# Columns 256 to 511 of x's first 512 rows: eight TensorE transposes replaced by one transposing DMA, and two broadcasts moved behind the Silu table

## Chip, cores and metric

The kernel runs on one core of a Trainium2 chip. The metric is the device time of one launch in microseconds (us). Its engines are TensorE (PE; its weight loads are shown as PEld), VectorE (DVE), ScalarE (ACT), GpSimd (POOL) and SyncE (SP). DMAs are issued from SP's and ACT's instruction queues and are moved by 16 DMA engines.

## What is computed

A gate mixes two branches over the same x (2048 rows of 448 columns, bf16): a diagonal complex state space model, and a dense layer pair with Silu.

```python
g = sigmoid((x * gate_w).sum(-1, keepdims=True))
# branch a
dt      = exp(log_dt)
Lam_bar = exp(dt * (Lambda_re + 1j * Lambda_im))
Bu      = einsum("bld,pd->blp", x, ((Lam_bar - 1) / Lam)[:, None] * Bmat)
h_t     = Lam_bar * h_{t-1} + Bu_t             # 2048 steps
a       = 2 * einsum("blp,dp->bld", h, Cmat).real + x * Dskip
# branch b
b = einsum("bsf,fd->bsd", silu(einsum("bsd,df->bsf", x, w1)), w2)   # 448 -> 1792 -> 448
out = g * a + (1 - g) * b
```

## The kernel before

Two successive rows of x are taken as one row of 896 columns (`x2`, 1024 rows): columns 0 to 447 are the even time steps, 448 to 895 the odd ones. The matmuls need x with its columns on partitions. That is `XT`, eight blocks of 128 columns by 1024 rows: blocks 0 to 3 for the even steps (block 3 holds columns 384 to 511, of which the lower 64 belong to the even steps), 4 to 7 for the odd ones. The recurrence is done on pairs of steps, and the w1 product ("ffn1") is done in four quarters of 512 rows (two of even steps, two of odd ones), each with 14 blocks of 128 hidden columns, written two PSUM banks at a time. Silu empties two banks at once into `AT` (L455).

The Tracker (L43) records every operation in program order, one list for each engine, and puts a wait on a semaphore ahead of an operation that reads or writes what another engine or a DMA has last touched. An engine's order is thus the order of the calls, and a waiting instruction holds up whatever stands behind it on its engine. The order is written by hand. DMAs to the keys R0 and R1 share one semaphore, and R2 has another.

The start, in which the change lies:

- **x, first 512 rows.** `XH` is their natural form, with four groups of 128 rows. SP and ACT load columns 0 to 255 of groups 0 and 1 (L276), then columns 0 to 383 of groups 2 and 3 (L280, keys XA2 and XA3), then the rest up to column 511 (keys XB0 and XB1, L282 and L286). PE turns 128x128 pieces (`turn_k`, L489 to L493; the instruction is L491) into PSUM, and DVE copies them to `XT` (L501, L507). So arise blocks 0 to 3 for rows 0 to 511. The eight turns of blocks 2 and 3 stand at L531 and L535.
- **Other XT blocks.** They come by transposing DMAs on SP (`ldt`, L228 and L229), from L309 on, behind a wait for the remainder rows of w1 (L308).
- **w1** goes to `W1E` in pieces: for the first 768 hidden columns by j (128 columns of x each, `ld_w`), a remainder of 64 rows (`ld_wr`), and the further columns (`ld_w3`).
- **Parameter rows.** log_dt, Lambda_re and Lambda_im are loaded into rows of `R` (L283; two from SP, one from ACT). DVE copies 64 columns to R's end (`rd`, L466). PE turns R into columns (`mm_cols`, L472), DVE copies them out to `PV` (L528), and from there come dt (L565, an Exp), two small DVE operations, `mag` (L569, another Exp), and, on ACT, a dummy Silu that loads the Silu table (L572). In the table of the profile such small operations are named by their helpers: L562 for ACT, L556 and L559 for DVE.
- **ffn1, first part.** `ffn1_first` (L427, matmuls at L433) does six hidden blocks in six banks, over j = 0, 1, 2. It is a generator that stops in between, so that turns stand among its matmuls; j = 2 comes last and reads block 2. `mm_cols` stands after three of the six matmuls of j = 1. Then come the remainders (`ffn1_rem`, L447), which read block 3 and `XR`, a copy of block 3's lower half in the upper partitions, each followed by a Silu of two banks (L455). After that ffn1 goes on in pairs through `lanes` (L365), the first of them in the two free banks, the next in the two that the first Silu empties.
- **Row broadcasts.** `ld_b` (L297) loads gate_w and Dskip to all partitions (`GWB`, `DB`), issued by ACT (L300, L301) behind a dummy Exp (L292) that loads the Exp table. They are first used in `gate` (L650) and `skip` (L658), where DVE multiplies x by them.
- **Natural x.** `load_xn(0)` (L303, SP) brings columns 512 to 895 of the first 512 rows.

Of the kernel before, what the change touches and what calls it, by code (L numbers as in the profile page):

```python
# [8 lines left out]
AF = mybir.ActivationFunctionType  # L9

F32 = DT.float32
BF16 = DT.bfloat16
# [138 lines left out]
def gated_mix(nc, A_x, A_Lambda_re, A_Lambda_im, A_B_re, A_B_im, A_C_re, A_C_im, A_log_dt,  # L151
              A_Dskip, B_x, B_w1, B_w2, gate_w, out):
    with ExitStack() as ctx:
        E = ctx.enter_context
        T = Tracker(nc, ctx)

        def sb(name, shape, dtype):
            return E(nc.sbuf_tensor(name, list(shape), dtype))

        x2 = A_x[0].rearrange("(k i) d -> k (i d)", i=2)  # L160
        out2 = out[0].rearrange("(k i) d -> k (i d)", i=2)

        XT = sb("XT", [128, 8, NK], BF16)
# [7 lines left out]
        XR = sb("XR", [128, NK], BF16)  # L171
# [4 lines left out]
        XN = sb("XN", [128, 2 * NKT * D], BF16)  # L176
        AT = [sb(f"AT{i}", [128, NFB, 512], BF16) for i in range(2)]
        OT = sb("OT", [128, 4, D], BF16)
        GWB = sb("GWB", [128, D], BF16)
        DB = sb("DB", [128, D], BF16)  # L180
        JK = sb("JK", [128, 2], BF16)
# [7 lines left out]
        ID = sb("ID", [128, 128], BF16)  # L189
# [5 lines left out]
        HP = sb("HP", [128, 1], F32)  # L195
# [25 lines left out]
        ps = E(nc.psum_tensor("ps", [128, 8, 512], F32))  # L221
# [3 lines left out]
        def ld(eng, dst, src, key, group=None):  # L225
            return T.dma(eng, lambda e: e.dma_start(dst, src), writes=[key], group=group)  # L226

        def ldt(dst, src, key, reads=(), group=None, also=()):  # L228
            return T.dma("sp", lambda e: e.dma_start_transpose(dst, src), reads=reads,  # L229
                         writes=[key, *also], group=group)  # L230
# [4 lines left out]
        def swap_xr(eng, h, odd):  # L235
            hs = slice(h * 512, (h + 1) * 512)
            if odd:
                T.op(eng, lambda e: e.tensor_copy(XR[0:64, hs], XT[64:128, 7, hs]), reads=XO[h][1],
                     writes=[f"XR{h}b"])
            else:  # L240
                T.op(eng, lambda e: e.tensor_copy(XR[64:128, hs], XT[0:64, 3, hs]), reads=XE[h][1],
                     writes=[f"XR{h}a"])
# [7 lines left out]
        def row(v):  # L250
            return v.rearrange("(o n) -> o n", o=1)

        XH = XN[:, 0:8 * D].rearrange("p (k c) -> p k c", k=4)
        XA = ["XA0", "XA1", "XA2", "XA3", "XB0", "XB1"]
        FA, FB = 768, 1280
        x0 = x2[0:512, 0:512].rearrange("(k p) c -> p k c", p=128)

        def ld_w(eng, j, f0=0, f1=FA, key=""):
            ld(eng, W1E[:, j, f0:f1], B_w1[j * 128:(j + 1) * 128, f0:f1], f"W1Ej{j}{key}")
# [4 lines left out]
        def ld_w3(eng, j0, j1, f0, f1, key):  # L264
            ld(eng, W1E[:, j0:j1, f0:f1], B_w1[j0 * 128:j1 * 128, f0:f1].rearrange("(j p) f -> p j f", p=128),
               f"W1E{key}{j0}")

        def ld_wr(eng, c, later):
            p = slice(64 * c, 64 * c + 64)
            if later:  # L270
                return ld(eng, W1E[p, 3, 384:896].rearrange("p (n f) -> p n f", n=2),
                          B_w1[384:448, FA:].rearrange("p (n c f) -> p n c f", n=2, c=2)[:, :, c, :], f"W1Es{c}")
            return ld(eng, W1E[p, 3, 0:384], B_w1[384:448, 384 * c:384 * c + 384], f"W1Er{c}")

        for k, eng in enumerate(("sp", "act")):
            ld(eng, XH[:, k, 0:256], x0[:, k, 0:256], XA[k])  # L276
        for c, eng in enumerate(("sp", "act")):
            ld_w(eng, 0, 384 * c, 384 * c + 384, c)
        for k, eng in ((2, "sp"), (3, "act")):
            ld(eng, XH[:, k, 0:384], x0[:, k, 0:384], XA[k])  # L280
        ld_w("sp", 1)
        ld("act", XH[:, 0:2, 256:512], x0[:, 0:2, 256:512], XA[4])  # L282
        for i, (eng, v) in enumerate((("sp", A_log_dt), ("sp", A_Lambda_re), ("act", A_Lambda_im))):  # L283
            ld_row(eng, i, v)
        ld_w("act", 2)
        ld("sp", XH[:, 2:4, 384:512], x0[:, 2:4, 384:512], XA[5])  # L286
        gE = [ld_wr(eng, c, False) for c, eng in enumerate(("sp", "act"))]
        ld_w3("sp", 0, 2, FA, FB, "d")
        ld_w3("act", 2, 3, FA, FB, "d")
        for c, eng in enumerate(("sp", "act")):  # L290
            ld_wr(eng, c, True)
        T.op("act", lambda e: e.activation(JK[:, 0:1], HP[:, :], AF.Exp), reads=["HP"], writes=["JK0"])  # L292
        ld_w3("sp", 0, 1, FB, F_FF, "e")
        ld_w3("act", 1, 3, FB, F_FF, "e")
        BTK = [f"BT{i}" for i in range(4)] + ["BTz"]
# [1 line left out]
        def ld_b(dst, src, key):  # L297
            ld("act", dst[:, :], row(src).partition_broadcast(128).rearrange("p o n -> p (o n)"), key)

        ld_b(GWB, gate_w, "GW")  # L300
        ld_b(DB, A_Dskip, "DB")  # L301

        def load_xn(h):  # L303
            c0 = 0 if h else 512
            ld("sp", XN[:, 8 * h * D:8 * (h + 1) * D].rearrange("p (k c) -> p k c", k=4)[:, :, c0:],
               x2[h * 512:(h + 1) * 512, c0:].rearrange("(k p) c -> p k c", p=128), f"XN{h}")

# [5 lines left out]
        for i, src in enumerate((A_B_re, A_B_im)):  # L313
# [15 lines left out]
             writes=["IOTA"])  # L329
# [128 lines left out]
        def ffn1(c, f0=0, ahead=None):  # L458
            for fb in range(f0, NFB, 2):
                pair(*ffn1_pair(c, fb), last=(c == 3 and fb == NFB - 2))  # L460
                if ahead and fb == 8:
                    ahead()
                yield
# [13 lines left out]
        def warm(n, b):  # L477
            def mm(pe):
                ins = None
                for _ in range(n):  # L480
                    ins = pe.matmul(ps[:, b, 0:128], ones, ones, start=True, stop=True)
                return ins
            T.op("pe", mm, writes=[f"ps{b}"])

        warm(NWARM, 5)
        PB = (6, 7, 6, 7)
        xp = [ps[:, b, 0:256].bitcast(BF16) for b in PB]

        def turn_k(j, k, b=None):  # L489
            b = PB[j] if b is None else b  # L490
            T.op("pe", lambda pe: pe.transpose(  # L491
                ps[:, b, 0:256].bitcast(BF16)[:, k * 128:(k + 1) * 128], XH[:, k, j * 128:(j + 1) * 128], ID[:, :]),
                reads=[XA[k if j < 2 or (j == 2 and k > 1) else 4 + k // 2], "ID"], writes=[f"ps{b}"])  # L493

        def turn_x(j, i):
            for k in (2 * i, 2 * i + 1):
                turn_k(j, k)
# [6 lines left out]
        def turned_x(j, i=None, b=None):  # L504
            c, key = (slice(0, 512), f"XTe0{j}") if i is None else (slice(256 * i, 256 * i + 256), f"XTe0{j}{i}")
            b = PB[j] if b is None else b
            T.op("dve", lambda e: e.tensor_copy(XT[:, j, c], ps[:, b, 0:256].bitcast(BF16)[:, c]),  # L507
                 reads=[f"ps{b}"], writes=[key])
# [13 lines left out]
        for k in (2, 3):  # L522
# [5 lines left out]
        T.op("dve", lambda e: e.tensor_copy(  # L528
            PV[:, :, :], ps[:, 7, 256:288].rearrange("p (t c) -> p t c", c=8)[:, :, 0:4]),
            reads=["pv", "ps7"], writes=["PV"])  # L530
        for i in range(2):  # L531
            turn_x(2, i)
        turned_x(2)
        next(first)
        for i in range(2):  # L535
            turn_x(3, i)

        names = {}

        def pc(n):  # L540
            if n not in names:
                names[n] = len(names)
            return names[n]

        def col(n):
            i = pc(n)
            return P[:, i, :]
# [7 lines left out]
        def pts(o, a, s1, s2, op0, op1, ra):  # L555
            T.op("dve", lambda e: e.tensor_scalar(col(o), a, s1, s2, op0, op1), reads=ra, writes=[o])  # L556

        def ptt(o, a, b, op, ra):
            T.op("dve", lambda e: e.tensor_tensor(col(o), a, b, op), reads=ra, writes=[o])  # L559

        def pact(o, a, f, ra, scale=1.0, bias=0.0):
            T.op("act", lambda e: e.activation(col(o), a, f, bias=bias, scale=scale),  # L562
                 reads=ra, writes=[o])
# [3 lines left out]
            col("phf"), LIM, 1.0 / TWO_PI, col("dt"), ALU.mult, ALU.mult), reads=["PV", "dt"], writes=["phf"])  # L567
        ptt("ar", col("dt"), LRE, ALU.mult, ["dt", "PV"])
        pact("mag", col("ar"), AF.Exp, ["ar"])  # L569
        turned_x(3)  # L570
        T.op("dve", lambda e: e.tensor_copy(XR[64:128, 0:512], xp[3][0:64, :]), reads=["ps7"], writes=["XR0a"])
        T.op("act", lambda e: e.activation(JK[:, 0:1], HP[:, :], AF.Silu), reads=["HP"], writes=["JK0"])  # L572
        pts("phr", col("phf"), MAGIC, -MAGIC, ALU.add, ALU.add, ["phf"])
        ptt("fr", col("phf"), col("phr"), ALU.subtract, ["phf", "phr"])
        pts("nfr", col("fr"), -1.0, None, ALU.mult, ALU.bypass, ["fr"])
# [6 lines left out]
            reads=["f2"] + SGN, writes=["f2s"])  # L582
# [55 lines left out]
        def xblock(b):  # L638
            v = XN[:, 4 * b * D:4 * (b + 1) * D].rearrange("p (k c) -> p k c", k=4) if b > 1 else \
                XH[:, :, b * D:(b + 1) * D]  # L640
            return v, [*(XA if b < 2 else []), *([f"XN{b // 2}"] if b else [])]

        def block(tile):
            return tile // 4 if tile > 7 else tile % 2
# [10 lines left out]
        def skip():  # L655
            for b in range(4):
                v, ks = xblock(b)
                T.op("dve", lambda e, v=v: e.tensor_tensor(  # L658
                    v, v, DB[:, :].unsqueeze(1).to_broadcast([128, 4, D]), ALU.mult),
                    reads=ks + ["DB"], writes=[f"XD{b}"] + ks)  # L660
                yield
# [12 lines left out]
             writes=["BTz"] + BTK[2:4])  # L674
# [486 lines left out]
        f = ffn1(2)  # L1161
# [100 lines left out]
```

## Time and profile before

| | us |
|---|---|
| three timed runs, median (lowest to highest) | 136.64 (136.61 to 136.76) |
| profiled execution | 136.72 |
| its span | 135.3 |
| PE busy | 131.9 (97%) |
| DVE busy | 114.2 (84%) |
| ACT busy | 93.7 (69%) |
| POOL busy | 15.1 (11%) |

The profile is of one execution. The span runs from its first to its last instruction, and times in the trace count from the span's start. A row gives start, length, engine, source line, operation, what is written and read, and in brackets how long the engine had been idle and what ended that. "SPq" and "ACTq" are the issue of a DMA from that queue; the time to landing counts from the start of the issue. "PEld" can run ahead of PE. The chain that ended last is followed back from the last instruction through whatever released each step. Matmul records are pipelined: the lengths of two may overlap, so in the chain only the part that pushes the end is counted.

### The profile page before, as it was taken

What the parts mean: (1) busy time and instruction counts of PE and PEld (TensorE: products, weight loads), DVE (VectorE), ACT (ScalarE), POOL (GpSimd) and SP (SyncE); (2) the same over time, 40 slices, a digit from 0 to 9 for tenths busy, and PEclk for the clock granted to TensorE, in tenths of its full rate; (3) what the DMA queues carried; (4) which work ended last, traced back from release to release, by engine and by line L of the source; (5) the groups of instructions that cost most, each with busy time, mean ns of one, the idle gap of its engine ahead of it and who ended that gap; (6) DMA issues with size and microseconds to landing.
All of it is one profiled execution on the core that took longest, in us unless ns stands there. A gap on an engine that the chain in (4) does not pass through costs nothing.

```text
span 135.3 us, 2630 instructions
## 1 busy us (share of the span) xinstructions
PE 131.9 (97%) x1072; PEld 65.7 (49%) x1073; DVE 114.2 (84%) x152; ACT 93.7 (69%) x146; POOL 15.1 (11%) x32
## 2 busy tenths in 40 slices
PE   7899999999999999999999999999999999999993
PEld 7554444444444554444445544445555555555552
DVE  1467898917899798999999999999999999994554
ACT  0369888899939999768999597797113437879200
POOL 7108768050000000000000000000000000000000
DMA  4999979999897220000122000000000000222123
GB/s 109 273 278 162 157 153 244 181 286 300 251 184 123 55 62 0 0 0 0 44 56 60 5 0 0 0 5 0 0 0 0 0 0 7 100 89 81 68 78 126
DMA packets 24928, 11.95 MB, mean 88 GB/s; under 512 B 16851, under 2 KB 24406, under 8 KB 24918
## 3 DMA queue, kind: packets, MB, share of 16 engines
q1 hardware_dynamic: 22996, 10.43, 32.3%
q10 hardware_dynamic: 1922, 1.37, 3.6%
q8 instruction: 8, 0.13, 0.4%
q14 instruction: 2, 0.02, 0.0%
HBM read 5.51 MB, written 1.84 MB: 54 GB/s over the span
## 4 chain that ended last, share of the span: by engine, by line
PE 94%; DMA 3%; DVE 1%; ACTq 1%; issue 0%
PE ps L365 44%; PE ps L794 16%; PE ps L809 16%; PE ps L1047 15%; DMA XN<-in_A_x_dram 3%; PE ps L433 3%; DVE TMPS L1071 1%; ACTq L226 1%; PE ps L491 1%; PE ps L447 1%; PE ps L472 0%
## 5 line engine op out<-in xcount | busy, mean ns | idle before, releaser
L365 PE MATMUL ps<-XT,W1E 64*128 64x512 bf16 x325 | 41.3, 376 | 0.0
L455 ACT ACTIVATE AT<-ps 128x1024 bf16<-128x1024 f32 x28 | 28.2, 1019 | 7.4 <-PE ps L365 7.2
L365 PEld LDWEIGHTS ps<-XT,W1E 64*128 64x128 bf16 x325 | 16.9, 94 | 19.0 <-ACT AT L455 0.3
L365 PE MATMUL ps<-XT,BT 64*128 64x512 bf16 x156 | 22.4, 376 | 0.0
L809 PE MATMUL ps<-W,AT 64*128 64x448 bf16 x224 | 21.5, 349 | 0.0
L794 PE MATMUL ps<-W,AT 128*128 128x448 bf16 x112 | 21.4, 353 | 0.0
L794 PEld LDWEIGHTS ps<-W,AT 128*128 128x128 bf16 x112 | 10.9, 98 | 10.5 <-issue 0.4
L809 PEld LDWEIGHTS ps<-W,AT 64*128 64x128 bf16 x224 | 10.9, 94 | 10.4
L838 ACT ACTIVATE BT<-ps,GT 128x448 bf16<-128x448 f32 x8 | 5.1, 634 | 13.2 <-PE ps L794 13.2
L894 DVE SCALAR_TENSOR_TENSOR HS<-VE,P,ps 128x512 bf16<-128x512 bf16 (+1 forms) x13 | 9.6, 780 | 3.9 <-PE ps L365 3.9
L365 PEld LDWEIGHTS ps<-XT,BT 64*128 64x128 bf16 x156 | 8.1, 94 | 9.3 <-DVE HS L894 0.4
L938 DVE TENSOR_TENSOR_SCAN G<-P,Q 128x1024 f32<-128x1024 f32 (+1 forms) x6 | 11.4, 1923 | 0.0
L1047 PE MATMUL ps<-CO,VE 128*128 128x448 bf16 (+2 forms) x63 | 11.1, 332 | 0.0
L1047 PE MATMUL ps<-CO,HS 128*128 128x448 bf16 x56 | 11.1, 352 | 0.0
L365 PE MATMUL ps<-XR,W1E 64*128 64x512 bf16 x25 | 9.2, 376 | 0.0
L1047 PEld LDWEIGHTS ps<-CO,VE 128*128 128x128 bf16 x63 | 6.0, 98 | 4.8
L1047 PEld LDWEIGHTS ps<-CO,HS 128*128 128x128 bf16 x56 | 5.5, 98 | 5.1
L891 DVE TENSOR_TENSOR Q<-G,COS 128x2048 bf16<-128x2048 f32 (+1 forms) x4 | 7.0, 1755 | 0.1
L891 DVE TENSOR_TENSOR Q<-G,SIN 128x2048 bf16<-128x2048 f32 (+1 forms) x4 | 7.0, 1750 | 0.0
L856 ACT ACTIVATE VE<-ps 128x1024 bf16<-128x1024 f32 x6 | 6.1, 1020 | 1.2 <-PE ps L365 1.2
L858 ACT ACTIVATE ps<-VE,P 128x1024 f32<-128x1024 bf16 x6 | 6.7, 1118 | 0.2
L894 DVE SCALAR_TENSOR_TENSOR VE<-HS,P,FP 128x512 bf16<-128x512 bf16 (+1 forms) x7 | 6.6, 976 | 0.1
(123 smaller groups left out, 179.1 us busy)
## 6 DMA issues: line engine op xcount, KB each, us to landing
W<-in_B_w_dram SPq DMA_DIRECT2D x2, 784.0 KB, 6.6
XN<-in_A_x_dram SPq DMA_DIRECT2D x1, 896.0 KB, 5.1
out_dram<-OT SPq DMA_DIRECT2D x8, 112.0 KB, 1.7
out_dram<-TMPS SPq DMA_DIRECT2D x7, 112.0 KB, 1.7
HS<-HS SPq DMA_DIRECT2D x4, 128.0 KB, 2.3
XN<-in_A_x_dram SPq DMA_DIRECT2D x1, 384.0 KB, 3.7
W1E<-in_B_w_dram SPq DMA_DIRECT2D x1, 256.0 KB, 5.5
W1E<-in_B_w_dram ACTq DMA_DIRECT2D x1, 256.0 KB, 5.0
```

The source lines that it names most:

```text
L365: ins = pe.matmul(ps[:, bank, :], w(p, j), xh(odd, h, j, p), start=start and j == js[0], stop=stop and j == js[-1], skip_group_check=seeded)
L433: T.op("pe", lambda pe, fb=fb, bank=bank, j=j, h=h, c=c: pe.matmul(ps[:, bank, c], W1E[:, j, ff(fb) * 128:(ff(fb) + 1) * 128], XT[:, j, c] ...
L455: T.op("act", lambda e: e.activation(a[:, fb:fb + n, :], ps[:, bank:bank + n, :], AF.Silu), reads=[f"ps{bank + i}" for i in range(n)], wri ...
L794: ins = pe.matmul(ps[:, bank, 0:D], a[:, fb, q * 128:(q + 1) * 128], W2[:, ff(fb), :], start=(first and fb == 0), stop=(fb == NFB - 1), sk ...
L809: ins = pe.matmul(ps[:, bank, 0:D], a[p, fb, q * 128:(q + 1) * 128], W2[p, ff(fb), :], start=(start and fb == 0), stop=(not start and fb = ...
L838: T.op("act", lambda e: e.activation(bs(tile), ps[:, bank, 0:D], AF.Copy, scale=sc), reads=[f"ps{bank}", "GT2" if h else "GRI"], writes=ks)
L856: T.op("act", lambda e: e.activation(VE[:, m:m + 2, hs], ps[:, b[0]:b[0] + 2, :], AF.Copy), reads=[f"ps{i}" for i in b], writes=vs)
L858: T.op("act", lambda e: e.activation(ps[:, o[0]:o[0] + 2, :], VE[:, m:m + 2, hs], AF.Copy, scale=c1("lr", pt)), reads=vs + ["lr"], writes= ...
L891: T.op("dve", lambda e: e.tensor_tensor(o, a, b, op), reads=reads, writes=writes)
L894: T.op("dve", lambda e: e.scalar_tensor_tensor(o, a, s, b, ALU.mult, ALU.add), reads=reads, writes=writes)
L938: T.op("dve", lambda e: e.tensor_tensor_scan(G[:, c, w], rb, Q1[:, c, w], init, ALU.mult, ALU.add), reads=[f"Q1{c}", "rr", f"G{c}"], write ...
L1047: ins = pe.matmul(ps[:, bank, c], state(kt, odd, m), CO[:, m, c], start=False, stop=(m == YB[-1]), skip_group_check=True)
```

## The change

Columns 256 to 511 of the first 512 rows no longer come by the loads XB0 and XB1 and the eight turns. One transposing DMA on SP writes blocks 2 and 3 of `XT` (two blocks by 512 columns) directly from x in memory. It stands behind the w1 piece of j = 1 and ahead of the two parameter rows that SP issues. The loads XA2 and XA3 shrink to columns 0 to 255; the natural form of columns 256 to 511 comes later, with `load_xn(0)`, so that the first block of `gate` and `skip` waits for that load too. `XR`'s copy is taken from `XT` instead of PSUM. On ACT the dummy Exp moves from behind the w1 loads of the remainder and of the columns 768 to 1279 to directly behind the piece of j = 2, and the two broadcasts move behind the dummy Silu.

```diff
-        XA = ["XA0", "XA1", "XA2", "XA3", "XB0", "XB1"]
+        XA = ["XA0", "XA1", "XA2", "XA3"]
...
         for k, eng in ((2, "sp"), (3, "act")):
-            ld(eng, XH[:, k, 0:384], x0[:, k, 0:384], XA[k])
+            ld(eng, XH[:, k, 0:256], x0[:, k, 0:256], XA[k])
         ld_w("sp", 1)
-        ld("act", XH[:, 0:2, 256:512], x0[:, 0:2, 256:512], XA[4])
+        ldt(XT[:, 2:4, 0:512], x2[0:512, 256:512], "XTe02", also=["XTe03"])
         for i, (eng, v) in enumerate((("sp", A_log_dt), ("sp", A_Lambda_re), ("act", A_Lambda_im))):
             ld_row(eng, i, v)
         ld_w("act", 2)
-        ld("sp", XH[:, 2:4, 384:512], x0[:, 2:4, 384:512], XA[5])
+        T.op("act", lambda e: e.activation(JK[:, 0:1], HP[:, :], AF.Exp), reads=["HP"], writes=["JK0"])
         gE = [ld_wr(eng, c, False) for c, eng in enumerate(("sp", "act"))]
...
-        T.op("act", lambda e: e.activation(JK[:, 0:1], HP[:, :], AF.Exp), reads=["HP"], writes=["JK0"])
...
-        ld_b(GWB, gate_w, "GW")
-        ld_b(DB, A_Dskip, "DB")
-
         def load_xn(h):
-            c0 = 0 if h else 512
+            c0 = 0 if h else 256
...
-        for i in range(2):
-            turn_x(2, i)
-        turned_x(2)
         next(first)
-        for i in range(2):
-            turn_x(3, i)
...
         pact("mag", col("ar"), AF.Exp, ["ar"])
-        turned_x(3)
-        T.op("dve", lambda e: e.tensor_copy(XR[64:128, 0:512], xp[3][0:64, :]), reads=["ps7"], writes=["XR0a"])
+        swap_xr("dve", 0, 0)
         T.op("act", lambda e: e.activation(JK[:, 0:1], HP[:, :], AF.Silu), reads=["HP"], writes=["JK0"])
+        ld_b(GWB, gate_w, "GW")
+        ld_b(DB, A_Dskip, "DB")
```

The rest follows from this: `PB` keeps banks 6 and 7 for blocks 0 and 1, `turn_k` waits for `XA[k]` alone, and `xblock(0)` waits for `XN0` as well.

## Prediction

> **What bounds the kernel now.** I read the chain that ended last first. The profiled execution took 136.72 us, of which 135.3 us are the span; the median of the three timed runs is 136.64, so 0.08 is taken off at the end. Seen whole, the chain says that TensorE (PE) sets the end:
>
> ```profile
> PE 94%; DMA 3%; DVE 1%; ACTq 1%; issue 0%
> ```
>
> In order of time, its first dozen microseconds look otherwise (start, length, what):
>
> ```profile
> 1.71 3.59 DMA XN<-in_A_x_dram
> 5.30 0.05 issue
> 5.34 0.23 PE ps L491
> 5.57 0.22 PE ps L433 x2
> 5.79 0.11 PE ps L491 x2
> 5.90 1.47 PE ps L433 x9
> 7.37 0.08 PE ps L472 x4
> 7.45 0.24 PE ps L491 x4
> 7.69 0.05 issue
> 7.75 0.59 PE ps L433 x2
> 8.34 0.22 PE ps L491 x4
> 8.56 1.29 PE ps L433 x6
> 9.86 0.76 PE ps L447 x6
> 10.61 31.76 PE ps L365 x294
> ```
>
> The eight transposes that go are the two "L491 x4" entries, 0.24 and 0.22 us. From 10.61 on there is no gap in PE until 132.76: a microsecond won or lost before that arrives whole at the end. So the question is only when the L365 stream can run.
>
> PE is not alone in deciding that. The timeline of the other engines (start, length, idle before it and what ended the idle time):
>
> ```profile
> 6.27 0.17 DVE L466 COPY R<-R 3x64 bf16<-3x64 bf16 x1
> 7.49 0.17 DVE L528 COPY PV<-ps 128x16 f32<-128x16 f32 x1 [1.04 <-PE ps L472]
> 7.69 0.21 ACT L562 ACTIVATE P<-PV 128x4 f32<-128x4 f32 x1 [0.58 <-DVE PV L528]
> 8.33 0.20 ACT L562 ACTIVATE P<-P 128x4 f32<-128x4 f32 x1 [0.43 <-DVE P L559]
> 8.56 1.28 ACT L572 ACT_TABLE_LOAD   x1
> 9.85 0.20 ACT L572 ACTIVATE JK<-HP 128x1 bf16<-128x1 f32 x1
> 10.22 1.94 ACT L455 ACTIVATE AT<-ps 128x1024 bf16<-128x1024 f32 x2 [0.17 <-PE ps L447]
> 11.30 1.19 PEld L365 LDWEIGHTS ps<-XT,W1E 64*128 64x128 bf16 x13 [0.32 <-ACT AT L455]
> ```
>
> This is a second path: three parameter rows land in R, DVE copies (6.27), PE turns them into columns (L472), PV, an Exp, two DVE operations, a second Exp, the Silu table load, and only then the first Silu that empties PSUM banks (10.22). PE's fifth ffn1 pair needs those two banks: its weights load at 11.30, released by ACT. ACT sat idle a mere 0.17 us ahead of 10.22. **The parameter path has 0.17 us of slack**, and the transposes that go lie behind L472, beside that path. What is taken from PE there can bring at most 0.17 us.
>
> **The change, part by part.**
>
> *Transposes and evacuations out.* PE loses 0.24 + 0.22 = 0.46 us of chain, DVE three copies of 0.42 us against a new one of 0.29 (the row of L241, which now fills the upper half of XR from XT). Worth up to 0.17 us by the slack above.
>
> *Smaller loads.* The third and fourth x loads fall from 96 to 64 KB, and 128 and 64 KB go. The fourth, issued at 1.71 and landed at 5.30, is on the chain; PE was idle 0.44 us for it. Between nothing and that 0.44 is won at PE; I take 0.2, provided nothing later binds.
>
> *The transposing load (T below) on SP.* The queue before:
>
> ```profile
> 2.16 0.43 SPq L226 DMA_DIRECT2D W1E<-in_B_w_dram  x1
> 2.64 0.33 SPq L226 DMA_DIRECT2D R<-in_A_log_dt_dram  x1
> 3.01 0.22 SPq L226 DMA_DIRECT2D R<-in_A_Lambda_re_dram  x1
> 3.27 0.41 SPq L226 DMA_DIRECT2D XN<-in_A_x_dram  x1
> 8.60 3.94 SPq L229 DMA_TRANSPOSE XT<-in_A_x_dram  x2
> ```
>
> T stands at 2.64, ahead of two of the three parameter rows and of four W1 loads. First its issue: 1.26 to 2.39 us each for the six into XT. T should take about 1.5, so the rows are issued at 4.2 and 4.5 in place of 2.64 and 3.01. Second, its data lie ahead of the rows. In this trace the loads of one queue land in the order of issue, and a small one waits for what precedes it: on SP the 192 KB of W1 issued at 2.16 land at 5.86, the 64 KB of x issued at 3.27 not before 7.27 (4.0 us, where the first 64 KB took 2.1), the 48 KB of W1 issued at 3.73 at 8.63. The DMA share is 0.94 to 1.00 from 2 to 10 us: nothing passes quickly.
>
> When do the rows land (call it t_R)? Before, by 6.27. **Low end:** issue at 4.2 plus the trace's shortest landing, 2.1: 6.3. **High end:** T at 2.64 plus the longest landing of a transposing load, 6.1, plus 0.3 for the rows behind it: 9.0. **Value:** the nearest row is the transposing load issued at 8.60 (384 KB), which also met some 2 us of ordinary loads ahead of it and landed after 5.6. T is two thirds as large but has more ahead of it, and ACT's loads share the engines until about 8. So T lands at 2.64 + 5.6 = 8.24, and I let the rows land with it. A second count: while the 64 KB of x (256 pieces of 256 bytes) moved alone on SP's side, from 5.86 to 7.27, ACT's queue got the larger part; if T's pieces are as small, it ends when ACT's queue (912 KB after the change) and SP's up to T (672 KB) have passed together, 1.62 MB, which the rates of the before trace reach at 7.9, plus half a microsecond to land: 8.4.
>
> The Trainium skill, "DMA: Bandwidth & Descriptors", section "Two DMAs through the same engine are not ordered", says that descriptors in one queue of one DMA engine start in order, while nothing orders the sixteen engines among each other. By it a row of 896 bytes could start only after T's share on its engine: t_R near 8.2; without it, 6.3. "Advanced Engine Details and Errata", section "X-Bar Transpose (TRN2)", holds transposing loads to be as fast as ordinary ones, which speaks for the change; the rows here are 4.0 us for a transposing load of 384 KB (issued at 23.00) against 3.7 for a plain one (19.01), but an issue of 1.26 to 2.39 against some 0.4, of which the page says nothing.
>
> *The path from t_R.* Durations of before, with PE's wait for its own turn (6.44 to 6.99) replaced by 0.06: from the start of the copy to the end of the dummy Silu 10.05 - 6.27 = 3.78, less 0.55, plus 0.06, gives 3.29. With 0.05 to start and 0.02 to the first Silu, that begins at t_R + 3.36 in place of 10.22: break-even at t_R = 6.86. At 8.24 it is 11.60, **1.38 us later**. PE's own path is shorter: t_R + 0.28 to load, 0.46 for L472, 0.65 for three matmuls of L433, 1.29 for six, 0.39 for the first remainder pair, 11.31. So ACT ends last, PE stalls at the two banks (11.30 becomes 12.68), and with no later gap in PE the 1.38 goes to the end. Both gains above disappear behind this wait.
>
> *Exp early, broadcasts behind the Silu table.* Exp's table (5.61 to 6.89) is no longer near the first Exp (7.69): no gain, it was covered. The two broadcasts take 0.49 + 0.45 us of ACT's queue, beside the 1.28 of the Silu table, as they and a W1 issue ran beside the Exp table before; uncovered they would cost up to 0.94 at the first Silu. Their data are wanted at 23.51 and 24.69, seven microseconds after they would land (10.3 + 5.9).
>
> *XN load.* 640 KB for 384 KB: 512 KB more took 1.4 us longer (5.1 for 896 KB against 3.7), so 0.7 later, 23.4, and the odd XT loads 0.7 later too. What waits is DVE (23.51, 27.52), which idles 3.22 us for PE before 31.03; uncovered it would be 0.7.
>
> *W1 behind T.* The remainder weights land up to 1 us later than 8.63, wanted at 9.79 before and at 10.9 after; the transposing loads that wait for them move equally, like PE. Nothing added.
>
> **Rivals.**
> *A, forecast:* rows behind T, 136.72 + 1.38 - 0.08 = 138.0; for t_R from 7.4 to 9.0, +0.54 to +2.14: 137.2 to 138.8.
> *B, the change pays:* the rows pass, t_R below 6.86, and T lands by about 8. Then 0.17 of slack plus 0.2 of earlier x: 136.3 (136.0 to 136.5). For it: they are tiny and issued by 4.7. Against it: the 4.0 us for 64 KB.
> *C, only T is late:* rows in time, L433's six wait for T. At 8.24 they begin at 8.34 against 8.56 before, so the 0.17 may be won; at 8.9 it is 0.44 lost. 136.5 to 137.1, middle 136.7.
> *D, the clock falls as well:* matmuls of 128 columns stood 0.115 us apart at the start (20 in 2.29) and 0.055 after 5.3 (4 in 0.22), though the records show 1.00 throughout. If a stall of 1.4 us brought the slow spacing back for the 4 us it lasted at first, 2 us more: 140. Against it: the 0.8 us of gaps between 4.2 and 5.4 did not prevent the change to the fast one. The skill's "TensorE: Matmul & The Clock Gate", Part 1, wants about 3.4 us of idleness for a fall, which would exclude D.
>
> **How the numbers follow.** A 0.72, B 0.10, C 0.10, D 0.08. Measurement here tells 0.2% (0.27 us) from nothing. Slower: nearly all of A (0.70), D, and 0.03 of C, 0.81. Faster: 0.08 of B, 0.03 of C, 0.11. Same: the rest, 0.08. The range leaves out most of B and D: 136.5 to 139.0.
>
> **What would show it.** Right: in the profile after, DVE's copy of R near 8.3, ended by a DMA; L472 just behind it; ACT's first Silu near 11.6, and the fifth pair's weights waiting for ACT at 12.7; L433's six not waiting for T. Wrong: the copy of R at or before 6.9 (B or C), a PE wait on XT's load ahead of L433's last six (C), matmuls 0.4 us apart where 512 columns took 0.22 (D), or a PE gap after 13 us, which would mean that XN or the transposed loads lost their cover.

## The result and the profile after

The changed kernel takes **138.30 us** (median of six executions, 138.18 to 140.22) against 136.62 for the kernel before, run on the same chip: a ratio of 1.0152, 95% interval 1.0122 to 1.0182. The ratio is not the quotient of the two medians (1.012): the ratios are formed from single executions, without those more than 1.5% above the fastest of their kernel. The forecast was 138.0. The profiled execution took 138.26 (136.72 before), its span 136.9. In the one execution of 140.22 the mean granted clock was 0.988 in place of 1.00; the experiments come back to that.

After the diff, line numbers in the changed kernel are lower by up to eleven: L365 is now L361, L433 L429, L447 L443, L455 L451, L466 L462, L472 L468, L528 L523, L572 L561.

Engines' shares of the chain that ended last, from the page of the changed kernel:

```profile
PE 91%; DMA 3%; SPq 3%; DVE 1%; issue 0%
```

Its beginning in order of time (start, length, what):

```profile
2.64 1.34 SPq L229
...
4.04 0.57 SPq L226
...
4.66 4.10 DMA R<-in_A_Lambda_re_dram
...
8.78 0.18 DVE R L462
...
9.10 0.24 PE ps L468 x4
...
9.41 1.89 PE ps L429 x8
11.30 0.75 PE ps L443 x6
12.06 31.87 PE ps L361 x294
```

Where the load of x and PE's first matmuls stood, there now stand the issue of the transposing load T, the issue of the two parameter rows behind it, and 4.10 us until the second of them has landed. Everything in the chain from 0.78 to 9.10 is SP's queue ahead of the rows, the rows themselves and DVE's copy of them.

The timeline, in the same columns as before:

```profile
8.78 0.17 DVE L462 COPY R<-R 3x64 bf16<-3x64 bf16 x1 [3.19 <-DMA R<-in_A_Lambda_re_dram]
...
9.10 0.24 PE L468 MATMUL ps<-ID,R 128*128 128x4 bf16 x4 [1.74 <-DVE R L462]
9.38 0.17 DVE L523 COPY PV<-ps 128x16 f32<-128x16 f32 x1 [0.42 <-PE ps L468]
...
11.69 0.21 ACT L561 ACTIVATE JK<-HP 128x1 bf16<-128x1 f32 x1
...
11.80 1.92 ACT L451 ACTIVATE AT<-ps 128x1024 bf16<-128x1024 f32 x2
...
11.89 1.02 PE L361 MATMUL ps<-XT,W1E 64*128 64x512 bf16 x7
...
12.86 1.19 PEld L361 LDWEIGHTS ps<-XT,W1E 64*128 64x128 bf16 x13 [0.43 <-ACT AT L451]
```

The copy of R waits 3.19 us for the DMA, where it had no wait before. The first Silu starts at 11.80 in place of 10.22 (+1.58) and has lost its idle time ahead: ACT, not PE, now comes last. The fifth pair's weights load at 12.86 in place of 11.30 (+1.56). From 12.06 on the chain shows no gap in PE, and its stream ends at 134.32 instead of 132.76: the same 1.56, carried through.

PE's own order is nearly as late. L468 stands ahead of the rest of L429 on PE, so PE waits 1.74 us for the copy of R, and the L361 stream starts at 11.89. In the profile before it started at 10.45:

```profile
10.45 1.02 PE L365 MATMUL ps<-XT,W1E 64*128 64x512 bf16 x7
```

So 1.44 us of the 1.56 have arisen on PE before it comes to the two banks, and ACT adds some 0.1. Both paths begin at the same rows.

### The profile page after: what moved, and what is told of

Same layout as the page of the kernel before. It is cut to its first block, busy times and chain, and to the rows that moved or that the text cites. A ratio compares the mean times of both kernels' runs of the same rounds, so it can differ in the third digit from the quotient of the medians.

```text
span 136.9 us, 2610 instructions
## 1 busy us (share of the span) xinstructions
PE 131.5 (96%) x1064; PEld 65.0 (48%) x1065; DVE 113.3 (83%) x150; ACT 93.6 (68%) x146; POOL 13.4 (10%) x32
## 4 chain that ended last, share of the span: by engine, by line
PE 91%; DMA 3%; SPq 3%; DVE 1%; issue 0%
PE ps L361 43%; PE ps L785 16%; PE ps L800 15%; PE ps L1038 15%; DMA R<-in_A_Lambda_re_dram 3%; SPq L226 2%; PE ps L429 1%; SPq L229 1%; DVE TMPS L1062 1%; PE ps L443 1%; PE ps L468 0%; DVE R L462 0%
## 5 line engine op out<-in xcount | busy, mean ns | idle before, releaser
L361 PE MATMUL ps<-XT,W1E 64*128 64x512 bf16 x325 | 41.5, 376 | 0.0
L451 ACT ACTIVATE AT<-ps 128x1024 bf16<-128x1024 f32 x28 | 28.2, 1018 | 7.3 <-PE ps L361 7.2
L361 PEld LDWEIGHTS ps<-XT,W1E 64*128 64x128 bf16 x325 | 16.9, 94 | 19.2 <-ACT AT L451 0.4
L361 PE MATMUL ps<-XT,BT 64*128 64x512 bf16 x156 | 22.4, 376 | 0.0
L361 PEld LDWEIGHTS ps<-XT,BT 64*128 64x128 bf16 x156 | 8.1, 94 | 9.3 <-DVE HS L885 0.3
L361 PE MATMUL ps<-XR,W1E 64*128 64x512 bf16 x25 | 9.2, 376 | 0.0
```

The costliest lines, as they stand in the source:

```text
L361: ins = pe.matmul(ps[:, bank, :], w(p, j), xh(odd, h, j, p), start=start and j == js[0], stop=stop and j == js[-1], skip_group_check=seeded)
L451: T.op("act", lambda e: e.activation(a[:, fb:fb + n, :], ps[:, bank:bank + n, :], AF.Silu), reads=[f"ps{bank + i}" for i in range(n)], wri ...
```

## Experiments

Two theories were to be told apart: **the rows** (the loss is the parameter path, late because its rows stand behind T) and **T's traffic** (T or the moved work on ACT would cost the time wherever the rows are). Each median stands beside that of the kernel before, run on the same chip; each profile is of one execution, and no trace of the others is kept.

### 1. Rows ahead of T

```diff
+        for i, (eng, v) in enumerate((("sp", A_log_dt), ("sp", A_Lambda_re), ("act", A_Lambda_im))):
+            ld_row(eng, i, v)
         ldt(XT[:, 2:4, 0:512], x2[0:512, 256:512], "XTe02", also=["XTe03"])
-        for i, (eng, v) in enumerate((("sp", A_log_dt), ("sp", A_Lambda_re), ("act", A_Lambda_im))):
-            ld_row(eng, i, v)
```

> The changed kernel with SP's two parameter rows issued ahead of the transposing load T. Rows theory (the whole loss is the parameter path, delayed by rows that land behind T): rows land before 6.5 as in the kernel before, the copy of R starts near 6.3, and T, issued 0.6 later, lands near 8.8 (8.1 in the changed kernel). Then the last six matmuls of the first part wait for T: they begin near 8.9 against 8.56 before and 10.0 in the changed kernel; first Silu near 10.6; 137.0 us (136.7 to 137.3). Rival, that T's traffic or the moved ACT work costs the time: no change, 138.3.

Measured: 139.49 us against 136.58, ratio 1.0181 (1.0136 to 1.0226), a clear miss. The rows did as expected: the copy of R starts at 6.76. But T, issued 0.63 us later than in the changed kernel, landed at 9.93, 1.8 us later. A PE row of the timeline, and then four of the trace's stretches of one microsecond (length, busy time and count of PE, PEld, DVE, ACT, POOL, then PE's granted clock, DMA share, GB/s):

```profile
10.07 1.71 PE L429 MATMUL ps<-XT,W1E 128*128 128x512 bf16 x6 [1.96 <-DMA XT<-in_A_x_dram]
```

```profile
10.00:11.00 1.00, 0.93 (x5) 0.49 (x6) 0.90 (x7) 0.00 (x0) 0.00 (x0) 1.00 1.13 333
11.00:12.00 1.00, 1.00 (x5) 0.15 (x5) 0.93 (x6) 0.00 (x0) 0.58 (x1) 0.56 1.00 260
12.00:13.00 1.00, 1.00 (x8) 0.33 (x6) 0.97 (x2) 0.64 (x1) 1.00 (x1) 0.50 0.80 123
13.00:14.00 1.00, 1.00 (x8) 0.41 (x6) 0.70 (x1) 1.00 (x2) 0.92 (x2) 0.50 1.07 221
```

The last six matmuls wait 1.96 us for T, and then the granted clock falls to half for some three microseconds (0.56, 0.50, 0.50, then 0.73). Three of the six executions had a mean clock of 0.988 and took 140.0 to 140.9; the three at 1.00 took 138.3 to 139.0. So T is the next thing to be late, and some executions pay for the clock besides. How idle PE was hardly tells which: from 6 to 10 us PE was busy 1.49 us here and 1.65 in the profile of the changed kernel, where the clock stayed at 1.00. Why T took 6.66 us to land here, and 5.5 in the changed kernel, is open.

### 2. Rows on ACT, T where the change put it

```diff
-(("sp", A_log_dt), ("sp", A_Lambda_re), ("act", A_Lambda_im))
+(("act", A_log_dt), ("act", A_Lambda_re), ("act", A_Lambda_im))
```

> The changed kernel with all three parameter rows issued by ACT ahead of w1's piece j = 2; T stays where it is. Rows theory: T lands at 8.1 as in the changed kernel, the rows land before 6.9, the last six matmuls begin near 8.2 against 8.56 before, and the parameter path sets the first Silu at 10.05 to 10.2; 136.5 us (136.3 to 136.8), so not slower than the kernel before. Rival, T's traffic: 138.3. Second rival, that the transposed loads behind T (XT's other blocks and BT, which landed 2 to 3 us later than before in the changed kernel) have lost their cover once PE is early again: a new PE gap between 16 and 32 us, 136.9 to 137.6.

Measured: 137.22 us (136.57 to 137.81) against 136.58, ratio 1.0044 (1.0025 to 1.0062). Only the queue of two tiny loads differs from the changed kernel, and 1.1 of its 1.7 us are gone. The chain of the profiled execution (136.57):

```profile
2.64 5.63 DMA XT<-in_A_x_dram
...
8.40 1.46 PE ps L429 x6
```

The copy of R starts at 6.96, and the chain now runs through T: landed at 8.27, the matmuls begin at 8.40 against 8.56 before. The rows land nearly when expected (by 6.9), but the median lies above the expected range (136.3 to 136.8) and fits the second rival, whose new PE gap between 16 and 32 us this profile does not have. That execution is the fastest of twelve; the others took up to 1.2 us more, and what held them up is open.

### 3. Rows behind an ordinary load, no T

```diff
-        for i, (eng, v) in enumerate((("sp", A_log_dt), ("sp", A_Lambda_re), ("act", A_Lambda_im))):
-            ld_row(eng, i, v)
+        ld_row("act", 2, A_Lambda_im)
         ld_w("act", 2)
         ld("sp", XH[:, 2:4, 384:512], x0[:, 2:4, 384:512], XA[5])
+        ld_w3("sp", 0, 2, FA, FB, "d")
+        for i, v in enumerate((A_log_dt, A_Lambda_re)):
+            ld_row("sp", i, v)
         gE = [ld_wr(eng, c, False) for c, eng in enumerate(("sp", "act"))]
-        ld_w3("sp", 0, 2, FA, FB, "d")
```

> The kernel before, no transposing load added, with SP's two parameter rows (and the w1 remainder piece after them) moved behind the ordinary 256 KB load of w1. Rows theory, order of a queue whatever kind of load stands ahead: the rows land near 9.3 (8.5 to 9.7), the copy of R starts there, the first Silu near 12.4, and the time rises by about 2.2 us to 138.8 (138.1 to 139.3). Rival, that only a transposing load holds back what follows it: the rows land by 7 as they are tiny, and the time stays at 136.6 to 136.8.

Measured: 137.89 us (136.83 to 138.77) against 136.58, ratio 1.0109 (1.0073 to 1.0145). Slower, but below the expected range (138.1 to 139.3) and above that of the rival. The profiled execution (136.83, the fastest) sides with the rival. The ordinary load, issued at 3.13 (size, us from issue to landing), and the second row:

```profile
W1E<-in_B_w_dram SPq DMA_DIRECT2D x1, 256.0 KB, 5.3
```

```profile
4.05 2.96 DMA R<-in_A_Lambda_re_dram
```

The load landed at 8.4, the row behind it at 7.01. "Lands in the order of issue" is no rule, then: here a single row was through 1.4 us ahead of a large load in front of it. What the slower executions did is open.

### 4. Rows issued late, nothing large ahead

```diff
-        for i, (eng, v) in enumerate((("sp", A_log_dt), ("sp", A_Lambda_re), ("act", A_Lambda_im))):
-            ld_row(eng, i, v)
+        ld_row("act", 2, A_Lambda_im)
         ld_w("act", 2)
         ld("sp", XH[:, 2:4, 384:512], x0[:, 2:4, 384:512], XA[5])
+        T._wait("sp", ["HSz3"], [])
+        for i, v in enumerate((A_log_dt, A_Lambda_re)):
+            ld_row("sp", i, v)
```

This is the kernel before, with the rows behind the 64 KB load of x and held until POOL's last memset, which ends at 4.20. POOL's operations are recorded ahead of the loads for it, in their old order.

> The kernel before, no transposing load added; SP's two parameter rows wait for POOL's last memset, so that they are issued near 4.25 and 4.6 as in the changed kernel (4.04 and 4.66), with only ordinary loads ahead of them. Two halves of the rows theory are told apart: in the changed kernel the rows land at 8.76, because they are issued 1.65 us later (T's issue takes 1.34 us and more) or because T's data are ahead of them. Late issue alone: landing 3.75 after the issue as with the rows first, near 8.4, and 137.9 us. T's data: landing some 2.5 to 3 after the issue, 7.1 to 7.6 (2.96 behind an ordinary load), and 136.7 to 137.2 us.

Measured: 137.10 us against 136.62, ratio 1.0040 (1.0022 to 1.0058). Its chain:

```profile
4.58 2.85 DMA R<-in_A_Lambda_re_dram
...
7.45 0.18 DVE R L468
```

Issued at almost the same time as in the changed kernel (4.58 and 4.66), the row takes 2.85 us to land without T and 4.10 behind it. The copy of R starts at 6.76 with the rows first, 7.45 when they are issued late, and 8.78 when they are also behind T. Of the delay, 0.7 us belong to the late issue, and 1.3 come with T ahead, put down to its data; of the time, 0.5 and about 1.2. Run 2 gave back 1.1 of these 1.7; what the rest is there, is open.

### 5. ACT's part alone, its halves, and the change without it

The kernel before with ACT's part alone (dummy Exp ahead of the four w1 loads, broadcasts behind the dummy Silu), in two runs on different chips; each half alone; and the changed kernel with that part undone, thus:

```diff
-        T.op("act", lambda e: e.activation(JK[:, 0:1], HP[:, :], AF.Exp), reads=["HP"], writes=["JK0"])
         gE = [ld_wr(eng, c, False) for c, eng in enumerate(("sp", "act"))]
...
+        T.op("act", lambda e: e.activation(JK[:, 0:1], HP[:, :], AF.Exp), reads=["HP"], writes=["JK0"])
         ld_w3("sp", 0, 1, FB, F_FF, "e")
...
+        ld_b(GWB, gate_w, "GW")
+        ld_b(DB, A_Dskip, "DB")
...
         T.op("act", lambda e: e.activation(JK[:, 0:1], HP[:, :], AF.Silu), reads=["HP"], writes=["JK0"])
-        ld_b(GWB, gate_w, "GW")
-        ld_b(DB, A_Dskip, "DB")
```

> The kernel before with only ACT's part of the change: the dummy Exp ahead of four w1 loads, the two broadcasts behind the dummy Silu. Rows theory: covered, 136.6 us (136.4 to 136.8), the first Silu at 10.2. Rival, that the broadcasts' issue delays the first Silu: up to 0.94 later, 137.5. The broadcasts now move beside the transposed loads of 9 to 16 us; if that slows these, BT and XT blocks land later than in the kernel before, without a PE gap as long as PE's need for BT comes after.

> The kernel before with only ACT's part of the change (dummy Exp and broadcasts), once more: each of the two alone made no difference (136.44 and 136.52 against 136.54), both together took 0.3% (interval 0.05 to 0.6%). If the two act together, 136.9 again; if that was chance, 136.5 to 136.6.

> The kernel before with the two broadcasts alone moved behind the dummy Silu. Broadcast theory: as with ACT's part as a whole, 136.9 us with some executions near 138, and in the profile a transposing load behind the remainder weights that takes over 7 us. Rival, that the early Exp did it: 136.6, spread as before.

> The kernel before with the dummy Exp alone moved ahead of the four w1 loads. Broadcast theory: no change, 136.6 us (136.4 to 136.8), the transposing loads land as before. Rival, that the early Exp did it: 136.9, executions near 138.

> The changed kernel with ACT's part undone, thus the transposing load T, the smaller x loads and the larger XN load alone. Rows theory: the rows still land behind T, near 8.8, and the time stays at 138.3 (138.0 to 138.6); the transposing loads of B land in some 5 us after their issue where the changed kernel took over 8, off the path. Rival, that the broadcasts carry a good part of the loss of the changed kernel: 137.6 or less.

| | us | beside | ratio (95%) |
|---|---|---|---|
| both halves on the kernel before | 136.94 | 136.58 | 1.0033 (1.0005 to 1.0061) |
| the same again | 136.87 | 136.62 | 1.0026 (0.9997 to 1.0056) |
| broadcasts behind the Silu only | 136.44 | 136.54 | 0.9997 (0.9980 to 1.0014) |
| early Exp only | 136.52 | 136.54 | 1.0000 (0.9986 to 1.0014) |
| change without ACT's part | 139.21 | 136.54 | 1.0202 (1.0169 to 1.0235) |

Three rows miss what was expected: both halves together lie a little above 136.4 to 136.8, the broadcasts alone, put at 136.9, cost nothing, and the change without ACT's part, put at 138.3, came out 0.9 higher, with a mean clock of 0.988 in two of its six executions (139.74 and 140.33). The issue of the broadcasts is covered by the Silu table, as the timeline of the changed kernel also has it (10.18 to 11.19, beside 10.40 to 11.68). Neither half costs anything, and of both together 0.3% may be true: in the profile of the first run a transposing load of XT took 8.4 us instead of 5.6 and PE waited for it near 16. With T in place ACT's part looks rather like a gain (1.0202 without it, 1.0152 with it, but the intervals overlap): without it the broadcasts move beside T and the w1 loads behind T, and in the profile one of these loads (64 KB) landed at 13.3, 7.2 us after its issue. PE's waits up to 16 us show it:

```profile
PE ps L364 <- DMA W1E<-in_B_w_dram: 0.7, 1, 0.7
```

### 6. Three tries to make T pay

All three keep the rows on ACT.

The first undoes ACT's part of the change besides.

> The changed kernel with all three parameter rows on ACT, and ACT's part of the change undone: the dummy Exp behind the w1 loads and the broadcasts behind it, as in the kernel before. Broadcast theory: what was left over the kernel before with the rows on ACT (137.2 against 136.6) comes from the broadcasts, which now move beside the transposing loads of 9 to 16 us and slow them (5.6 us to land for the first of these before, 6.4 with the rows on ACT, 8.4 with ACT's part alone); undone, 136.5 us (136.2 to 136.8), and a spread as narrow as that of the kernel before. Rival: T itself lands earlier or later from run to run, and the last six matmuls of the first part wait for it: 137.2 again, with the same spread.

The second starts from run 2; the third is the second with the two broadcasts moved on, behind `run(ffn1(0, NF1 + 2))`:

```diff
-        ld_w3("act", 1, 3, FB, F_FF, "e")
...
         T.op("act", lambda e: e.activation(JK[:, 0:1], HP[:, :], AF.Silu), reads=["HP"], writes=["JK0"])
+        ld_w3("act", 1, 3, FB, F_FF, "e")
         ld_b(GWB, gate_w, "GW")
         ld_b(DB, A_Dskip, "DB")
```

> The changed kernel with the three rows on ACT, and ACT's last w1 load (256 KB, columns 1280 and up) behind the dummy Silu, ahead of the broadcasts: less traffic beside T. If ACT's loads take the engines from T, T lands before 7.9 instead of 8.27, the last six matmuls begin near 8.0, and the slack of 0.17 us ahead of the first Silu is won: 136.3 us (136.1 to 136.7) against 136.55 before. Rival, that T's landing is set by its own issue and length: 8.2 to 8.4, and 136.7 to 137.2 as before with the rows on ACT. Third: the w1 load comes too late for the hidden blocks 10 to 13 (wanted near 13.6), 137 and more.

> The kernel of the last run with the rows on ACT and ACT's last w1 load behind the dummy Silu, with the two broadcasts moved further, behind the Silus of the first ffn1 quarter (about 15 to 16 us; their data are wanted from 23.5 on). If the broadcasts beside the transposing load of XT's rows 512 to 1023 made that one land after 7.3 us and PE stall 0.5 us near 15.7 there, it lands within some 6 us and the stall is gone: first Silu near 10.0, no PE gap after 10.3, 136.2 us (136.0 to 136.6), a little under the kernel before. Rival, that this load is slow without the broadcasts too, or T's landing swings from run to run: 136.7 to 137.1 as with the broadcasts at the Silu table.

Measured: 136.72 (136.02 to 137.79) against 136.54, ratio 1.0023 (0.9998 to 1.0048); 137.06 against 136.62, 1.0032 (1.0008 to 1.0057); 136.58 (136.00 to 137.85) against 136.56, 1.0016 (0.9989 to 1.0044). None beats the kernel before. The first still ranged from 136.02 to 137.79, so the old place of the broadcasts did not narrow the spread, as its theory had said. The second had one execution of 140.62 with a mean clock of 0.988. The second's first Silu came at 9.96, 0.26 us earlier than before, and the gain was lost again near 15.7, where PE waited for the transposing load of XT's further rows:

```profile
PEld ps L360 <- DMA XT<-in_A_x_dram: 0.5, 1, 0.5
```

From issue to landing the load in question, the first of two, took, in the second and in the third, where the broadcasts stay away from it:

```profile
XT<-in_A_x_dram SPq DMA_TRANSPOSE x1, 7.3
```

```profile
XT<-in_A_x_dram SPq DMA_TRANSPOSE x1, 4.8
```

The third's profiled execution has no such gap, a first Silu at 9.62, and 136.00 us, below every run of the kernel before in this study. But the other executions reach 137.85 where those of the kernel before, beside it, lie between 136.15 and 136.95. In the four profiles with the rows on ACT the time goes with T's landing: 7.6 us and 136.00, 7.9 and 136.50, 8.3 and 136.57 (run 2), 8.3 and 136.66. That the slower executions are those in which T lands later still is likely, but not shown.

## Why the prediction was right

- **What is late: shown; for whom: a near tie.** The copy of R waits for a DMA, the first Silu moves by 1.58 us (forecast 1.38), PE's fifth pair by as much, and nothing later gives it back. The forecast had PE's own path ready 0.29 us ahead of ACT's and PE stalling at the two banks for the whole 1.38; measured, PE's path was some 0.13 ahead (the second pair of L443's matmuls starts at 11.46, and in the profile before the first Silu could follow 0.20 after that pair's start), and PE had waited already, at L468. The number does not depend on it, as both paths start at t_R. Taking the rows out from behind T took back 1.1 us (run 2).
- **T and t_R.** T was put at 8.24 and landed at 8.1. The rows were put at the same 8.24; they landed at 8.76. This term was 0.5 too small. Its two halves are now measured (run 4): 0.7 us for the late issue (T's own took 1.34, 1.5 was forecast), and 1.3 behind T. The second count, 8.4, rests on a wrong reading: from 5.86 to 7.27 of the trace before, SP's queue moved 0.19 MB and ACT's 0.17, so the 64 KB of x did not move alone and ACT's queue did not get the larger part; and no run shows its half microsecond to land.
- **Path from t_R.** Put at 3.36 us, measured 11.80 - 8.76 = 3.04. The weights and matmuls of L468 took 0.31 in place of 0.50 once PE stood waiting, and the first Silu began 0.11 after the start of the dummy one, not 0.22. Two errors, +0.52 and -0.32, so that the sum came within 0.2: that closeness is luck.
- **The reason given for t_R was too simple.** "The loads of one queue land in the order of issue" fails in run 3, where a row overtook the load ahead of it. The Trainium skill, "DMA: Bandwidth & Descriptors", section "Two DMAs through the same engine are not ordered", has it better: order of starting within one engine's queue, none among engines. The rows behind T (4.10 us, 2.85 without it) fit its first half; run 3 (2.96 us behind an ordinary load of 256 KB) fits its second. Which engines carried the rows is not on record, so neither half is shown.
- **Both gains disappear: right.** PE's transposes are gone and nothing came of it. With the rows on ACT the first Silu started up to 0.6 us earlier than before, and even then the median was no better. The early Exp brought nothing, as forecast (136.52 against 136.54 in run 5).
- **Rival C** was real but hidden: in the changed kernel T lands before PE gets to it; in the profile of run 1 it is, with the clock, the whole loss. I priced it up to 0.44; the executions there with the clock at 1.00 lost 1.7 to 2.4 (138.3 to 139.0).
- **Rival D** was priced well at some 2 us and excluded too readily. The mean clock was 0.988 in one of six executions of the changed kernel, in three of six of run 1 and in two of six of the change without ACT's part. "TensorE: Matmul & The Clock Gate", Part 1, asks for some 3.4 us of idleness; in run 1 PE's longest wait was 1.96 us, within 4 us (6 to 10) of which it was busy 1.49.
- **XN right, what stands ahead of it overlooked.** 0.7 us more was expected of XN's load, and it took 4.5 us to land in place of 3.7. But the first two loads of B, ahead of it in the queue, took 8.5 and 8.1 us (4.9 and 5.1 before), so that XN was issued at 21.06 in place of 19.01. DVE's idle time ahead of the recurrence's first operation fell from 3.22 to 0.81 us, although PE came 1.56 later. The cover held, with little to spare.

## What to carry to other kernels

Before a load is put into a queue, look at what is issued behind it: two rows of 896 bytes decided here, and moving them to the other queue was worth more than all that the load replaced. When an engine is relieved, find the second path that ends at the same place and its slack (0.17 us here); that is the most that can be won while the second path stays where it is. And a load that matmuls wait for at a busy start has to be judged by the spread of many executions: the kernel with the best single one (136.00 us) ranged over 1.85 us, the kernel before, beside it, over 0.8. The spread is not the change's alone: on another chip two of 29 executions of the kernel before took 138.4 and 138.7.

## Not expected of the hardware

- Two broadcasts of 112 KB beside transposing loads: 4.8 us to land became 7.3 for the same load (third and second try of 6). These are two single executions, and in run 1 this load took 4.8 too, with the broadcasts under way until 13.5, so they are not shown to be the cause. In the changed kernel the DMA engines moved 64 GB/s between 13 and 15 us at a share of 1.05, with broadcasts and transposing loads under way.
- A transposing load issued 0.63 us later landed 1.8 us later (run 1), with only two rows between.
- The granted clock fell to 0.50 for some three microseconds after a wait of 1.96 us.
